# Transposing the rotated q and k by DMA instead of on TensorE, in a gated linear attention with a gated MLP

## Chip, cores, metric

The kernel runs on one core of a Trainium2 chip. The metric is the device time of one execution in microseconds (us), and lower is better. A ratio is the mean time of one kernel's fast runs over the mean time of the fast runs of the kernel before in the same rounds, so it is not quite the ratio of the medians that stand beside it. Profiled executions give "spans", which are about 2 us shorter than the times of the same executions (338.0 against 339.8 us before); shares of a period and the positions of instructions come from them.

## The reference, cut to what matters

The first part is a linear recurrence with complex decay over 768 steps, for 4 batches and 8 heads of width 48. The second part is a gated MLP over the 3072 resulting tokens.

```python
for t in range(S):                                   # S = 768
    S_re, S_im = ar*S_re - ai*S_im + kv, ar*S_im + ai*S_re
    y[:, :, t] = einsum('bhd,bhde->bhe', q[:, :, t], S_re)
x = y as (3072, 384)
out = (sigmoid(x @ w_gate) * (x @ w_val)) @ w_out    # 384 -> 1536 -> 384
```

The kernel works on chunks ("slabs") of 128 tokens of one batch, 24 in all. In a slab the recurrence becomes attention with a triangular mask: q and k are scaled by the accumulated decay and rotated by the accumulated phase, and a score matmul of k by q follows. That matmul contracts over the head's coordinates, so it wants q and k with those coordinates on the partitions, whereas the rotation leaves tokens on the partitions. Hence the transposes.

## The kernel before

Slabs are grouped into ten blocks of 1, 2, 3, 3, 3, 3, 3, 3, 2 and 1. The loads of block i+2, the preparation of block i+1, the attention of block i, the gate matmuls of block i-1 and the output matmuls of block i-2 are interleaved by hand. ACT's order is the program's. A scheduler, which knows only estimated times, decides the order in which the other engines' and the DMA queue's instructions stand. On each engine, and on the SyncE queue that issues the DMAs, instructions then go in that order.

```python
SIZES = [1, 2, 3, 3, 3, 3, 3, 3, 2, 1]

def prep_b(g):                       # rotation: kst and qst of each slab
    ...
        for i, dst in enumerate((ks, qs)):
            nc.vector.tensor_tensor(out=dst..., in0=G.qk[:, 1 - i, s]..., in1=cs..., op=ALU.mult)
        G.qs.append(qs); G.ks.append(ks)

def turn(s, hf):                     # in attn(g): four heads of q and k
    tp = ps_gen.tile([L, 8, L], F16, tag="gen")
    for i in range(4):
        h = hf * 4 + i
        nc.tensor.transpose(tp[:, 4 + i], G.ks[s][:, h], idn_t)
        nc.tensor.transpose(tp[:, i], G.qs[s][:, h], idn_t)
    qkT = patt.tile([L, 8, L], F16, tag="qkT", bufs=5)
    nc.vector.tensor_copy(out=qkT, in_=tp)

def score(s, hf): ...                # reads qkT: sc, then mask
...
for i in range(NG + 2):              # one stage per block
    if i + 2 < NG:
        loads_a(i + 2); loads_q(i + 2)      # 15 DMAs of 192 KB for a block of 3 slabs
    st = [attn(i) first part, outproj(i - 2), prep_a(i + 1)];            merge(*st)
    st = [attn(i) rest, gateval(i - 1), prep_b(i + 1), prep_0(i + 2)];   merge(*st)
```

(Cut and, in the last four lines, shortened.) All loads, and in the changed kernel all DMA transposes, are issued by SyncE. The weights are loaded by GpSimd through another DMA queue.

Of the kernel before, what the change touches and what calls it, by code (L numbers as in the profile page):

```python
# [17 lines left out]
YSC = 2.0**10  # L18
# [4 lines left out]
def kernel(  # L23
# [58 lines left out]

    def cload(shape, dt, src, name):
        t = const.tile(shape, dt, name=name)
        nc.sync.dma_start(t, src.ap())
        return t


    class Grp:
# [22 lines left out]
                    dst.rearrange("t (h d) -> t h d", d=D),  # L112
                    src[b, :, c * L:(c + 1) * L].rearrange("h t d -> t h d"))

    loads_a(0)
    wl_t = cload([L, L], F32, wl_d, "wl_t")
    wt_t = cload([L, L], F32, wt_d, "wt_t")
    on_t = cload([L, L], F32, on_d, "on_t")
    idn_t = cload([L, L], F16, idn_d, "idn_t")
    nid_t = cload([L, L], F16, nid_d, "nid_t")  # L120
    msk_t = cload([L, L], F32, msk_d, "msk_t")
    loads_q(0)
    pio2 = const.tile([L, 1], F32, name="pio2")
    nc.vector.memset(pio2, np.pi / 2)

# [33 lines left out]
    def prep_0(g):  # L159
        G = gs[g]  # L160
        n = len(GROUPS[g])
        G.lm = pa.tile([L, NS, HD], F32, name=f"lm_{g}", tag="lm")
        sq = pa.tile([L, 2, NS, HD], F32, name=f"sq_{g}", tag="sq", bufs=1)
        nc.scalar.activation(out=sq[:, :, :n], in_=G.a2[:, :, :n],  # L164
                             func=FT.Square)
        for s in range(n):
            nc.gpsimd.tensor_tensor(out=G.lm[:, s], in0=sq[:, 0, s],  # L167
                                    in1=sq[:, 1, s], op=ALU.add)
            nc.gpsimd.tensor_scalar(out=G.lm[:, s], in0=G.lm[:, s],
                                    scalar1=CAP, scalar2=-1.0,  # L170
                                    op0=ALU.min, op1=ALU.max)
            yield
        for s in range(n):
            nc.gpsimd.tensor_scalar(out=G.v16[:, s], in0=G.v32[:, s],  # L174
                                    scalar1=YSC, scalar2=1.0,
                                    op0=ALU.mult, op1=ALU.mult)
        yield

    def prep_a(g):
        G = gs[g]  # L180
        n = len(GROUPS[g])
        ar, ai = G.a2[:, 0, :n], G.a2[:, 1, :n]
        lm = G.lm[:, :n]
        nc.scalar.preload_act_table_set("natural_log_exp_and_others")  # L184
        nc.scalar.activation(out=ar, in_=ar, func=FT.Ln)
        nc.scalar.activation(out=lm, in_=lm, func=FT.Ln)
        nc.scalar.activation(out=ar, in_=ar, func=FT.Exp, scale=-1.0)  # L187
        for s in range(n):
            G.last_pool = nc.gpsimd.tensor_tensor(  # L189
                out=G.a2[:, 1, s], in0=G.a2[:, 1, s], in1=G.a2[:, 0, s],  # L190
                op=ALU.mult)
        yield
        for s, (b, c) in enumerate(GROUPS[g]):
            ee = pe_.tile([L, 2, HD], F32, name=f"ee_{g}_{s}", tag="ee")
            cl = ps_gen.tile([L, HD], F32, name=f"cl_{g}_{s}", tag="gen")
            nc.tensor.matmul(cl, wl_t, G.lm[:, s], start=True, stop=True)  # L196
            nc.scalar.activation(out=ee[:, 0], in_=cl, func=FT.Exp,
                                 scale=0.5)
            nc.scalar.activation(out=ee[:, 1], in_=cl, func=FT.Exp,  # L199
                                 scale=-0.5)  # L200
            nc.sync.dma_start(scr[b][c:c + 1], ee[L - 1:L, 0])
            with nc.allow_non_contiguous_dma(reason="column of decays"):
                for p0 in (0, 64):
                    nc.sync.dma_start(
                        rbe[b][p0:p0 + D, c],
                        scr[b][c].rearrange("(h d) -> d h", d=D))
            if c > 0:
                nc.vector.tensor_tensor(
                    out=arr[b][:, c - 1], in0=rbe[b][:, c - 1],
                    in1=rbe[b][:, c], op=ALU.mult)  # L210
            nc.gpsimd.tensor_tensor(out=G.qk[:, :, s], in0=G.qk[:, :, s],  # L211
                                    in1=ee, op=ALU.mult)
            yield

    def prep_b(g):
        G = gs[g]
        n = len(GROUPS[g])
        th = G.a2[:, 1]
        nc.scalar.preload_act_table_set("sigmoid_and_others")
        nc.scalar.activation(out=th[:, :n], in_=th[:, :n], func=FT.Arctan)  # L220
        nc.scalar.preload_act_table_set("silu_and_others")
        G.qs, G.ks = [], []
        yield
        for s, (b, c) in enumerate(GROUPS[g]):
            ct = ps_gen.tile([L, HD], F32, name=f"ct_{g}_{s}", tag="gen")
            nc.tensor.matmul(ct, wt_t, th[:, s], start=True, stop=False,  # L226
                             skip_group_check=True)
            if c > 0:
                nc.tensor.matmul(ct, on_t, run[b], start=False, stop=False,  # L229
                                 skip_group_check=True)  # L230
            if c < NCH - 1:
                nr = psm.tile([L, HD], F32, name=f"run_{g}_{s}", tag="run")
                if c == 0:
                    nc.gpsimd.tensor_copy(out=nr, in_=th[:, s])
                else:
                    nc.gpsimd.tensor_tensor(out=nr, in0=run[b], in1=th[:, s],
                                            op=ALU.add)
                run[b] = nr
            r16 = psm.tile([L, HD], F16, name=f"r16_{g}_{s}", tag="r16")
            nc.vector.tensor_scalar(out=r16, in0=ct, scalar1=RCONST,  # L240
                                    scalar2=-RCONST, op0=ALU.add, op1=ALU.add)
            nc.tensor.matmul(ct, nid_t, r16, start=False, stop=True,
                             skip_group_check=True)
            yield
            cs = pcs.tile([L, 2, HD], F32, name=f"cs_{g}_{s}", tag="cs")
            nc.scalar.activation(out=cs[:, 0], in_=ct, func=FT.Abs)
            nc.scalar.activation(out=cs[:, 1], in_=ct, func=FT.Sin,
                                 scale=TWO_PI)
            nc.scalar.activation(out=cs[:, 0], in_=cs[:, 0], func=FT.Sin,  # L249
                                 scale=-TWO_PI, bias=pio2)  # L250
            qs, ks = slots[(FIRST[g] + s) % NSLOT]
            for i, dst in enumerate((ks, qs)):
                nc.vector.tensor_tensor(  # L253
                    out=dst.rearrange("p h (r x) -> p h r x", r=2)[:, :, :, 0:D],
                    in0=G.qk[:, 1 - i, s].rearrange("p (h d) -> p h d", d=D)
                    .unsqueeze(2).broadcast_to([L, H, 2, D]),
                    in1=cs.rearrange("p r (h d) -> p h r d", d=D),
                    op=ALU.mult)
            G.qs.append(qs)
            G.ks.append(ks)  # L260
            yield
# [4 lines left out]
    def attn(g):  # L266
# [28 lines left out]
                    nc.vector.tensor_copy(out=pn, in_=kv)  # L295
                P[b] = pn

        def turn(s, hf):
            tp = ps_gen.tile([L, 8, L], F16, name=f"tp_{g}_{s}_{hf}",
                             tag="gen")  # L300
            for i in range(4):
                h = hf * 4 + i
                nc.tensor.transpose(tp[:, 4 + i], G.ks[s][:, h], idn_t)  # L303
                nc.tensor.transpose(tp[:, i], G.qs[s][:, h], idn_t)  # L304
            qkT = patt.tile([L, 8, L], F16, name=f"qkT_{g}_{s}_{hf}",
                            tag="qkT", bufs=5)
            nc.vector.tensor_copy(out=qkT, in_=tp)  # L307
            Q[s].append(qkT)

        def score(s, hf):  # L310
            qkT = Q[s][hf]
            sc = ps_gen.tile([L, 4, L], F32, name=f"sc_{g}_{s}_{hf}",
                             tag="gen")
            for i in range(4):
                nc.tensor.matmul(sc[:, i], qkT[:, 4 + i], qkT[:, i],  # L315
                                 start=True, stop=True)
            mst = patt.tile([L, 4, L], F16, name=f"mst_{g}_{s}_{hf}",
                            tag="mst", bufs=5)
# [6 lines left out]
        def yout(s):  # L325
            b, c = GROUPS[g][s]
            y = ps_gen.tile([L, H, D], F32, name=f"y_{g}_{s}", tag="gen")
            for h in range(H):
                if c > 0:
                    nc.tensor.matmul(y[:, h], Q[s][h // 4][:, h % 4],  # L330
                                     X[s][:, h], start=True, stop=False)
                nc.tensor.matmul(y[:, h], M[s][h // 4][:, h % 4], V[s][:, h],  # L332
                                 start=(c == 0), stop=True)
# [11 lines left out]

        for s in range(n + 1):
            if s < n:
                turn(s, 0)
                yield
                turn(s, 1)  # L350
                yield
                state(s)
                yield
# [68 lines left out]
        return len(GROUPS[g])  # L422

    with tc.manual_schedule(engines={ACT}):
        run_all(prep_0(0))
        run_all(prep_a(0))
        loads_a(1)
        loads_q(1)
        with tc.issue_after(gs[0].last_pool.ins):
            load_weights()  # L430
        run_all(prep_b(0))
        run_all(prep_0(1))
        for i in range(NG + 2):
            st = []
            if i + 2 < NG:
# [1 line left out]
                loads_q(i + 2)  # L437
            if i < NG:
                at = attn(i)
                na = 7 * sz(i)  # L440
                n1 = na * 2 // 5
                st.append((take(at, n1), n1))
            if 0 <= i - 2:
# [9 lines left out]
            if i + 1 < NG:  # L453
                st.append((prep_b(i + 1), 1 + 2 * sz(i + 1)))
            if i + 2 < NG:
                st.append((prep_0(i + 2), 1 + sz(i + 2)))
            merge(*st)
# [1 line left out]
_INS = ['q', 'k', 'v', 'a_re', 'a_im', 'moe_w_gate', 'moe_w_val', 'moe_w_out']  # L459
# [26 lines left out]
```

## Time and profile before

339.7 us (median; 339.17 to 340.0).

| | before |
|---|---|
| span | 338.0 us |
| TensorE busy | 268.2 us |
| VectorE / ACT / GpSimd busy | 211.5 / 221.9 / 161.6 us |
| busy time of the DMA queue of SyncE, over 16 engines | 51.7% of the span |

The page's busy line, and two rows of its 40 slices of 8.45 us (tenths of busy time):

```profile
PE 268.2 (79%) x2328; PEld 175.5 (52%) x2328; DVE 211.5 (63%) x385; ACT 221.9 (66%) x377; POOL 161.6 (48%) x177
...
PE   0414073549778997989899989998999999999995
...
DMA  6999999991894199539813960383023100100110
```

The start is bound by loads: DMA at 9 tenths and TensorE mostly idle for about seven slices. From slice 11 or so on TensorE is nearly full. The table of windows says the same in numbers; its columns are the stretch, its length, then each engine's busy time with the number of instructions (PE, weight loads, VectorE, ACT, GpSimd), TensorE's granted clock, the DMA share and GB/s:

```profile
0.00:57.00 57.00, 17.64 (x90) 9.60 (x90) 14.02 (x30) 28.02 (x36) 31.33 (x42) 0.85 1.17 175
...
121.00:154.00 33.00, 29.77 (x257) 18.62 (x256) 25.53 (x45) 25.77 (x43) 20.71 (x23) 1.00 0.76 125
...
187.00:221.00 34.00, 31.66 (x276) 20.07 (x275) 24.86 (x46) 25.73 (x43) 18.84 (x19) 1.00 0.59 101
```

(The DMA share adds up the packets' times, so it can exceed 1.) In the steady stage a period handles one block of three slabs: TensorE is busy 29.8 of 33 us, ACT 25.8. What the transposes cost is less plain. The view of the tile tp, into which the transposes write (in PSUM, the memory for TensorE's results), lists its instructions (duration of one in ns, minimum/median/maximum, first and last start in us, then the forms):

```profile
L303 PE MATMUL tp<-idn_t,kst x192: 216/219/314, 19.0 to 314.7; 128*128 128x128 f16 x192
L304 PE MATMUL tp<-idn_t,qst x192: 217/219/314, 19.9 to 314.7; 128*128 128x128 f16 x192
L307 DVE COPY qkT<-tp x48: 675/688/692, 20.8 to 315.0; 128x1024 f16<-128x1024 f16 x48
```

384 records of 219 ns would be 84 us, but the records overlap. The windows, asked for the tile tp alone, give the time in which at least one of them ran: 33.14 us.

```profile
0.00:338.00 338.00, 33.14 (x384) 32.38 (x48) 0.94 0.59 97
```

ACT's order is fixed by the program, and each block's decay preparation begins there with a table load. These loads are the "marks", and a "stage" runs from one mark to the next; stage i holds the attention of block i. Three marks of the kernel before, from its timeline (start us, us, engine, line):

```profile
52.86 1.28 ACT L184 ACT_TABLE_LOAD   x1
...
90.06 1.28 ACT L184 ACT_TABLE_LOAD   x1
...
256.35 1.28 ACT L184 ACT_TABLE_LOAD   x1
```

They open stages 1, 2 and 7.

### The profile page before, as it was taken

What the parts mean: (1) busy time and instruction counts of PE and PEld (TensorE: products, weight loads), DVE (VectorE), ACT (ScalarE), POOL (GpSimd) and SP (SyncE); (2) the same over time, 40 slices, a digit from 0 to 9 for tenths busy, and PEclk for the clock granted to TensorE, in tenths of its full rate; (3) what the DMA queues carried; (4) which work ended last, traced back from release to release, by engine and by line L of the source; (5) the groups of instructions that cost most, each with busy time, mean ns of one, the idle gap of its engine ahead of it and who ended that gap; (6) DMA issues with size and microseconds to landing.
All of it is one profiled execution on the core that took longest, in us unless ns stands there. A gap on an engine that the chain in (4) does not pass through costs nothing.

```text
span 338.0 us, 6365 instructions
## 1 busy us (share of the span) xinstructions
PE 268.2 (79%) x2328; PEld 175.5 (52%) x2328; DVE 211.5 (63%) x385; ACT 221.9 (66%) x377; POOL 161.6 (48%) x177
## 2 busy tenths in 40 slices
PE   0414073549778997989899989998999999999995
PEld 0102042236556664656566656565666666666874
DVE  2021027528883985797679647966797798476633
ACT  4664067566689489749785977597757865774443
POOL 2880197957189519924873487247602630300000
PEclk9999559759796999999999999999999999999999
DMA  6999999991894199539813960383023100100110
GB/s 141 150 191 186 197 186 131 181 148 26 117 174 63 25 172 186 88 64 186 150 28 64 185 134 19 66 163 57 2 47 95 26 0 20 54 2 23 48 44 28
DMA packets 152382, 32.70 MB, mean 97 GB/s; under 512 B 144904, under 2 KB 152352, under 8 KB 152352
## 3 DMA queue, kind: packets, MB, share of 16 engines
q1 hardware_dynamic: 148368, 28.76, 51.7%
q0 software_dynamic: 3984, 3.54, 6.5%
q8 instruction: 18, 0.29, 0.4%
q14 instruction: 12, 0.10, 0.1%
HBM read 31.07 MB, written 4.76 MB: 106 GB/s over the span
## 4 chain that ended last, share of the span: by engine, by line
PE 48%; ACT 19%; DMA 10%; DVE 7%; POOL 6%; issue 5%; SPq 3%; DVEq 0%; ACTq 0%; POOLq 0%
PE pg L373 10%; PE pv L378 9%; PE po L392 9%; DMA v<-in_v_dram 5%; PE cl L196 4%; PE ct L226 4%; DMA a<-in_a_im_dram 3%; POOL qk L211 3%; PE ct L229 3%; ACT sq L164 2%; ACT g L381 2%; PE tp L304 2%; PE tp L303 2%; DVE qst L253 2%; ACT L184 2%
## 5 line engine op out<-in xcount | busy, mean ns | idle before, releaser
L373 PE MATMUL pg<-xt,wg 128*128 128x384 f16 (+2 forms) x360 | 68.0, 296 | 7.9 <-ACT g L381 5.7
L378 PE MATMUL pv<-xt,wv 128*128 128x384 f16 (+2 forms) x360 | 68.9, 297 | 3.6 <-DVE p L382 2.8
L381 ACT ACTIVATE g<-pg 128x384 f16<-128x384 f32 (+2 forms) x120 | 49.5, 429 | 33.6 <-PE pg L373 29.8
L382 DVE SCALAR_TENSOR_TENSOR p<-g,pv 128x384 f16<-128x384 f16 (+2 forms) x120 | 54.4, 467 | 20.8 <-ACT g L381 17.0
L392 PE MATMUL po<-wo,p 128*128 128x384 f16 x288 | 55.2, 326 | 0.0
L307 DVE COPY qkT<-tp 128x1024 f16<-128x1024 f16 x48 | 32.4, 687 | 33.6 <-PE tp L304 33.3
L373 PEld LDWEIGHTS <-wg 128*128 128x128 f16 x360 | 31.9, 98 | 25.3 <-issue 14.8
L211 POOL TENSOR_TENSOR qk<-qk,ee 128x768 f32<-128x768 f32 x24 | 43.6, 1837 | 2.8 <-ACT ee L199 2.6
L226 PE MATMUL ct<-a,wt_t 128*128 128x384 f32 x48 | 24.6, 599 | 24.0 <-ACT a L220 23.9
L240 DVE TENSOR_SCALAR r<-ct 128x384 f16<-128x384 f32 x24 | 13.2, 551 | 48.3 <-PE ct L229 29.0
L378 PEld LDWEIGHTS <-wv 128*128 128x128 f16 x360 | 32.4, 98 | 19.1 <-issue 7.1
L196 PE MATMUL cl<-lm,wl_t 128*128 128x384 f32 x48 | 24.1, 593 | 19.0 <-DMA qk<-in_k_dram 9.3
L319 DVE TENSOR_TENSOR mst<-sc,msk_t 128x512 f16<-128x512 f32 x48 | 32.4, 684 | 8.3 <-PE sc L315 8.1
L189 POOL TENSOR_TENSOR a<-a 128x384 f32<-128x384 f32 x24 | 23.8, 1015 | 28.7 <-ACT a L187 28.6
L174 POOL TENSOR_SCALAR v<-v 128x384 f16<-128x384 f32 x24 | 15.5, 644 | 43.2 <-PE y L332 25.8
L167 POOL TENSOR_TENSOR lm<-sq 128x384 f32<-128x384 f32 x24 | 25.9, 1095 | 17.6 <-ACT sq L164 17.0
L392 PEld LDWEIGHTS <-p 128*128 128x128 f16 x288 | 26.2, 98 | 13.8 <-issue 0.7
L303 PE MATMUL tp<-idn_t,kst 128*128 128x128 f16 x192 | 29.8, 230 | 2.9 <-DVE kst L253 2.9
L304 PE MATMUL tp<-idn_t,qst 128*128 128x128 f16 x192 | 29.2, 229 | 1.8 <-DVE qst L253 1.8
L285 POOL CAST x<-u 128x384 f16<-128x384 f32 x20 | 11.3, 569 | 33.9 <-DVE u L279 21.4
L253 DVE TENSOR_TENSOR kst<-qk,cs 128x768 f16<-128x768 f32 x24 | 23.7, 988 | 5.4 <-ACT cs L249 4.9
L253 DVE TENSOR_TENSOR qst<-qk,cs 128x768 f16<-128x768 f32 x24 | 26.8, 1119 | 0.0
(54 smaller groups left out, 490.3 us busy)
## 6 DMA issues: line engine op xcount, KB each, us to landing
a<-in_a_re_dram SPq DMA_DIRECT2D x24, 192.0 KB
a<-in_a_im_dram SPq DMA_DIRECT2D x24, 192.0 KB
qk<-in_q_dram SPq DMA_DIRECT2D x24, 192.0 KB
qk<-in_k_dram SPq DMA_DIRECT2D x24, 192.0 KB
v<-in_v_dram SPq DMA_DIRECT2D x24, 192.0 KB
out_dram<-ot SPq DMA_DIRECT2D x24, 192.0 KB
wg<-in_moe_w_gate_dram POOLq DMA_DIRECT2D x3, 384.0 KB, 7.1
wv<-in_moe_w_val_dram POOLq DMA_DIRECT2D x3, 384.0 KB, 8.6
```

Source lines behind the costliest of these rows:

```text
L196: nc.tensor.matmul(cl, wl_t, G.lm[:, s], start=True, stop=True)
L211: nc.gpsimd.tensor_tensor(out=G.qk[:, :, s], in0=G.qk[:, :, s], in1=ee, op=ALU.mult)
L226: nc.tensor.matmul(ct, wt_t, th[:, s], start=True, stop=False, skip_group_check=True)
L253: nc.vector.tensor_tensor(out=dst.rearrange("p h (r x) -> p h r x", r=2)[:, :, :, 0:D], in0=G.qk[:, 1 - i, s].rearrange("p (h d) -> p h d" ...
L303: nc.tensor.transpose(tp[:, 4 + i], G.ks[s][:, h], idn_t)
L304: nc.tensor.transpose(tp[:, i], G.qs[s][:, h], idn_t)
L307: nc.vector.tensor_copy(out=qkT, in_=tp)
L373: nc.tensor.matmul(pg, wg16[:, j, fc], G.xt[:, j, :nt], start=(j == 0), stop=(j == 2))
L378: nc.tensor.matmul(pv, wv16[:, j, fc], G.xt[:, j, :nt], start=(j == 0), stop=(j == 2))
L381: nc.scalar.activation(out=g16, in_=pg, func=FT.Tanh, scale=0.5)
L382: nc.vector.scalar_tensor_tensor(out=G.p[:, fb, :nt], in0=g16, scalar=1.0, op0=ALU.add, in1=pv, op1=ALU.mult)
L392: nc.tensor.matmul(po, G.p[:, fb, s * L:(s + 1) * L], wo16[:, fb], start=(fb == 0), stop=(fb == NFB - 1))
```

## The change

The intent: take 384 matmuls from the engine that binds, and 48 copies of 0.69 us from VectorE, and give the work to the DMA engines, which are idle for long stretches in the later part. In addition, the loads of block 1 go ahead of the weights, and the cast of v moves by a stage.

```diff
-        def turn(s, hf):
-            tp = ps_gen.tile([L, 8, L], F16, ...)
-            for i in range(4):
-                h = hf * 4 + i
-                nc.tensor.transpose(tp[:, 4 + i], G.ks[s][:, h], idn_t)
-                nc.tensor.transpose(tp[:, i], G.qs[s][:, h], idn_t)
-            qkT = patt.tile([L, 8, L], F16, ..., bufs=5)
-            nc.vector.tensor_copy(out=qkT, in_=tp)
+        def turn(s):
+            for x, src in ((1, G.ks[s]), (0, G.qs[s])):
+                t = patt.tile([L, H, L], F16, ..., tag=f"qkT{x}", bufs=3)
+                nc.sync.dma_start_transpose(
+                    out=t, in_=src.rearrange("p h x -> p (h x)"))
+                Q[s].insert(0, t)
...
     with tc.manual_schedule(engines={ACT}):
+        nc.scalar.preload_act_table_set("natural_log_exp_and_others")
+        loads_a(0)
+        consts()
+        loads_q(0)
+        loads_a(1)
+        loads_q(1)
         run_all(prep_0(0))
         run_all(prep_a(0))
-        loads_a(1)
-        loads_q(1)
-        with tc.issue_after(gs[0].last_pool.ins):
-            load_weights()
         run_all(prep_b(0))
         run_all(prep_0(1))
+        with tc.issue_after(gs[1].last_pool.ins):
+            load_weights()
```

(Cut: the cast of v from `prep_0` to `prep_b`, score and yout reading the new tiles, step counts; `consts()`, which now issues the loads of the constants; and `last_pool`, which now marks the last GpSimd instruction on a block's squares instead of its decay products.)

More of the change, by code (lines that the diff above doesn't have):

```diff
@@ L84, in cload, with consts @@
         t = const.tile(shape, dt, name=name)
-        nc.sync.dma_start(t, src.ap())
+        CONSTS.append((t, src))
         return t
+    CONSTS = []
+    def consts():
+        for t, src in CONSTS:
+            nc.sync.dma_start(t, src.ap())
     class Grp:
@@ L113, in loads_q @@
                     src[b, :, c * L:(c + 1) * L].rearrange("h t d -> t h d"))
-    loads_a(0)
     wl_t = cload([L, L], F32, wl_d, "wl_t")
@@ L121 @@
     msk_t = cload([L, L], F32, msk_d, "msk_t")
-    loads_q(0)
     pio2 = const.tile([L, 1], F32, name="pio2")
@@ L168, in prep_0 @@
                                     in1=sq[:, 1, s], op=ALU.add)
-            nc.gpsimd.tensor_scalar(out=G.lm[:, s], in0=G.lm[:, s],
+            G.last_pool = nc.gpsimd.tensor_scalar(
+                                    out=G.lm[:, s], in0=G.lm[:, s],
                                     scalar1=CAP, scalar2=-1.0,
@@ L172, in prep_0 @@
             yield
-        for s in range(n):
-            nc.gpsimd.tensor_scalar(out=G.v16[:, s], in0=G.v32[:, s],
-                                    scalar1=YSC, scalar2=1.0,
-                                    op0=ALU.mult, op1=ALU.mult)
-        yield
     def prep_a(g):
@@ L188, in prep_a @@
         for s in range(n):
-            G.last_pool = nc.gpsimd.tensor_tensor(
+            nc.gpsimd.tensor_tensor(
                 out=G.a2[:, 1, s], in0=G.a2[:, 1, s], in1=G.a2[:, 0, s],
@@ L222, in prep_b @@
         G.qs, G.ks = [], []
+        for s in range(n):
+            nc.gpsimd.tensor_scalar(out=G.v16[:, s], in0=G.v32[:, s],
+                                    scalar1=YSC, scalar2=1.0,
+                                    op0=ALU.mult, op1=ALU.mult)
         yield
@@ L296, in state @@
                 P[b] = pn
-        def turn(s, hf):
-            tp = ps_gen.tile([L, 8, L], F16, name=f"tp_{g}_{s}_{hf}",
-                             tag="gen")
-            for i in range(4):
-                h = hf * 4 + i
-                nc.tensor.transpose(tp[:, 4 + i], G.ks[s][:, h], idn_t)
-                nc.tensor.transpose(tp[:, i], G.qs[s][:, h], idn_t)
-            qkT = patt.tile([L, 8, L], F16, name=f"qkT_{g}_{s}_{hf}",
-                            tag="qkT", bufs=5)
-            nc.vector.tensor_copy(out=qkT, in_=tp)
-            Q[s].append(qkT)
+        def turn(s):
+            for x, src in ((1, G.ks[s]), (0, G.qs[s])):
+                t = patt.tile([L, H, L], F16, name=f"qkT_{g}_{s}_{x}",
+                              tag=f"qkT{x}", bufs=3)
+                nc.sync.dma_start_transpose(
+                    out=t, in_=src.rearrange("p h x -> p (h x)"))
+                Q[s].insert(0, t)
         def score(s, hf):
-            qkT = Q[s][hf]
             sc = ps_gen.tile([L, 4, L], F32, name=f"sc_{g}_{s}_{hf}",
@@ L314, in score @@
             for i in range(4):
-                nc.tensor.matmul(sc[:, i], qkT[:, 4 + i], qkT[:, i],
+                h = 4 * hf + i
+                nc.tensor.matmul(sc[:, i], Q[s][1][:, h], Q[s][0][:, h],
                                  start=True, stop=True)
@@ L329, in yout @@
                 if c > 0:
-                    nc.tensor.matmul(y[:, h], Q[s][h // 4][:, h % 4],
+                    nc.tensor.matmul(y[:, h], Q[s][0][:, h],
                                      X[s][:, h], start=True, stop=False)
@@ L347, in attn @@
             if s < n:
-                turn(s, 0)
-                yield
-                turn(s, 1)
+                turn(s)
                 yield
@@ L439 @@
                 at = attn(i)
-                na = 7 * sz(i)
+                na = 6 * sz(i)
                 n1 = na * 2 // 5
@@ L455 @@
             if i + 2 < NG:
-                st.append((prep_0(i + 2), 1 + sz(i + 2)))
+                st.append((prep_0(i + 2), sz(i + 2)))
             merge(*st)
```

## The prediction

> **What bounds it now.** The table of windows shows two stages. From 0 to 57 us the DMA engines are saturated (about 175 GB/s) and TensorE is busy only 17.6 us; the chain of waits runs there through loads: the v load of block 1, stretched by the weight loads to 18.4 us (19.4 to 37.8), then VectorE/GpSimd preparation, then a_im of block 2 (42.7 to 47.3). From about 90 us TensorE binds: busy 29.8, 31.1, 31.7 and 33.0 us in periods of 33, 33, 34 and 35 us (121 to 256), against ACT 25 to 26, DVE 25 to 27, GpSimd 16 to 21. (A period is three slabs.)
>
> **Removed.** 384 TensorE transposes and 48 VectorE copies of 687 ns. The groups credit the transposes with 59 us, but their two lines overlap: the windows of that tile alone sum to 33.1 us. So about 4.1 us of TensorE and 4.1 us of VectorE per period go.
>
> **Added.** 48 SBUF-to-SBUF transposes of 256 KB (128x1024, 2 bytes) on the SyncE queue. No trace here has one. The Trainium skill, "DMA: Bandwidth & Descriptors", Latency and other measured facts, gives 261 GB/s for a DMA transpose: estimate 1.0 us each, like the 1.0 us that a 192 KB load occupies here. "VectorE: DVE Perf Modes", The three transpose paths, gives 1309 ns for one 128x128 block, so eight blocks may well take more; my own middle estimate is 1.5 to 3 us of queue time each. Per period that is 9 to 18 us beside a DMA share of 0.6 to 0.76 (20 to 25 us of 33). The queue issues in order, and the built program puts twelve loads between the first and later transposes of a block, so scores of slabs 1 and 2 can wait. DMA or its queue will be nearly full until the loads end at about 240 us, and free afterwards.
>
> **Moved.** Weights start after block 1's squares, not after block 0's preparation: block 1 should have v and q by about 18 us rather than 41. Block 2's loads then meet the weights, so its a lands perhaps only 3 to 5 us earlier than 47. The v cast moves one stage later (about neutral).
>
> **On the critical path.** Start: 5 to 9 us. Steady stage: six full periods and the smaller ones could give 25 to 30 us if TensorE stayed the bound; I expect half or less, because DMA, its in-order queue or ACT (26 us busy plus handovers) takes over: periods of 30 to 32 us while loads run, 29 to 30 after. The last block exposes one transpose latency.
>
> Sum: 340 − 7 − 12 + 3 = about 324 us. Range 300 to 352. Faster by over 2%: 0.60; within: 0.21; slower: 0.19.
>
> **What would show each step.** TensorE busy falls by 30 to 36 us; DVE by 32. The page's DMA share in the middle slices rises to 8 or 9 tenths until about slice 28. Waits: the score matmuls' weight loads wait for a DMA (none now), some microseconds each. The first ct of block 1 starts near 20 us, not 44.
>
> **What would make it wrong.** If a transpose takes 1 us or less with its issue, TensorE keeps its bound and the time is near 305. If it takes over 4 us, or the SyncE queue spends that long issuing it, six per period plus 27 other transfers exceed 33 us, loads come late, and the kernel is slower, past 350. If the scheduler's order makes TensorE wait behind late scores (in-order engine), the saved 4 us come back as waits.

## The result, and the profile after

349.18 us (median; 348.97 to 349.9) against 339.7 us: ratio 1.0284, 95% interval 1.0264 to 1.0305. The result is correct, and the kernel is slower by 2.8%. The granted TensorE clock is not the cause: it was 0.902 in the profiled run of the change and 0.939 before, but the change's three other runs had 0.949 to 0.951 and still took 348.97 to 349.34 us.

The page after, the same three lines:

```profile
PE 247.8 (71%) x1944; PEld 155.2 (45%) x1944; DVE 179.1 (51%) x337; ACT 220.3 (63%) x377; POOL 159.8 (46%) x177
...
PE   0330002534686598869996998699989999999996
...
DMA  6999999998239989987997599839937923500500
```

TensorE lost 268.2 - 247.8 = 20.4 us of work and VectorE 32.4 us, so the intent was met. But TensorE now has a hole in slices 4 to 6, and the stages show when time was lost. The same marks, after:

```profile
66.94 1.28 ACT L184 ACT_TABLE_LOAD   x1
...
108.23 1.28 ACT L184 ACT_TABLE_LOAD   x1
...
271.58 1.28 ACT L184 ACT_TABLE_LOAD   x1
```

By the mark at the head of stage 2 the change is 108.23 - 90.06 = 18.2 us behind. From there to the head of stage 7 it takes 163.4 us where the kernel before took 166.3, so it wins back 2.9. From there to the end it takes 76.5 in place of 81.7 and wins 5.1 more. The three add up to the difference of the spans, 10.1 us.

So the steady stage is not the place. The list of TensorE's waits (waiter, what ended the wait, us in total, times, longest) names the new one; no score matmul waited for a DMA before:

```profile
PE sc L315 <- DMA qkT<-qst: 45.6, 6, 33.0
```

One wait of 33 us. The chain of waits through it, in order of time (start, us, what; SPq is SyncE's queue issuing, L105 and L117 are loads, L306 a transpose):

```profile
24.12 5.53 SPq L105
...
29.75 6.15 SPq L117
...
35.94 5.06 SPq L117
...
41.05 4.25 SPq L117
...
53.35 2.05 SPq L306
...
55.46 3.13 DMA qkT<-qst
...
58.63 0.58 PE sc L315 x4
```

And the rotated k and q of block 0 had been ready since 18.5 us, by the timeline of VectorE (in brackets its wait before, and for what):

```profile
16.68 0.96 DVE L257 TENSOR_TENSOR kst<-qk,cs 128x768 f16<-128x768 f32 x1 [2.04 <-ACT cs L253]
17.55 0.95 DVE L257 TENSOR_TENSOR qst<-qk,cs 128x768 f16<-128x768 f32 x1
```

They waited 35 us to be transposed, because the queue had the fifteen loads of block 2 to issue first. Four of these took 4 to 6 us each, while the weights were being loaded (their packets move from 23.7 to 47.9 us in the trace); the last five before the transposes took about 1 us each. The second transpose itself, once issued at 55.46, was there 3.1 us later. Meanwhile TensorE stood before the scores of block 0 and did not do the phase matmuls of block 1 that stand behind them: ACT had finished their input at 31.5 us, and they ran at 59.0, right after the first scores. This trace shows TensorE taking its matmuls in order.

The Trainium skill, "DMA: Bandwidth & Descriptors", Anatomy of one DMA, says where such a wait sits: the DMA engines do not wait on semaphores, and any wait happens on the issuing sequencer before it hands the DMA over. (The section describes DMAs that GpSimd issues; these are SyncE's.) This trace agrees: SyncE's own list of waits has 51.4 us of transposes waiting for the rotation of k, and everything behind them on the queue waits along. In the order of one queue a load can hold up a transpose, and a transpose can hold up a load.

### The profile page after: what moved, and what is told of

The parts are those of the page before. It is cut to its first block, busy times and chain, and to the rows that moved or that the text cites. A ratio compares the mean times of both kernels' runs of the same rounds, so it can differ in the third digit from the quotient of the medians.

```text
span 348.1 us, 5629 instructions
## 1 busy us (share of the span) xinstructions
PE 247.8 (71%) x1944; PEld 155.2 (45%) x1944; DVE 179.1 (51%) x337; ACT 220.3 (63%) x377; POOL 159.8 (46%) x177
## 2 busy tenths in 40 slices
DMA packets 203068, 45.24 MB, mean 130 GB/s; under 512 B 195592, under 2 KB 203040, under 8 KB 203040
## 3 DMA queue, kind: packets, MB, share of 16 engines
q1 hardware_dynamic: 199056, 41.35, 72.5%
## 4 chain that ended last, share of the span: by engine, by line
PE 41%; ACT 22%; SPq 14%; DVE 8%; issue 7%; DMA 7%; DVEq 0%; ACTq 0%
PE pv L376 8%; SPq L117 8%; PE pg L371 8%; PE po L390 7%; PE ct L230 5%; PE cl L196 4%; DMA qkT<-qst 3%; PE ct L233 3%; SPq L306 2%; ACT L219 2%; SPq L105 2%; ACT L184 2%; ACT g L379 2%; ACT L379 2%; DVE qst L257 2%
## 5 line engine op out<-in xcount | busy, mean ns | idle before, releaser
L371 PE MATMUL pg<-xt,wg 128*128 128x384 f16 (+2 forms) x360 | 70.3, 303 | 16.5 <-ACT g L379 11.0
L376 PE MATMUL pv<-xt,wv 128*128 128x384 f16 (+2 forms) x360 | 70.1, 302 | 2.4 <-ACT ot L396 1.4
L379 ACT ACTIVATE g<-pg 128x384 f16<-128x384 f32 (+2 forms) x120 | 48.4, 428 | 24.4 <-PE pg L371 21.6
L319 DVE TENSOR_TENSOR mst<-sc,msk_t 128x512 f16<-128x512 f32 x48 | 32.7, 684 | 52.3 <-PE sc L315 52.2
L315 PE MATMUL sc<-qkT,qkT 128*128 128x128 f16 x192 | 19.3, 229 | 45.6 <-DMA qkT<-qst 45.6
L390 PE MATMUL po<-wo,p 128*128 128x384 f16 x288 | 51.3, 326 | 0.0
L371 PEld LDWEIGHTS <-wg 128*128 128x128 f16 x360 | 33.5, 100 | 35.8 <-issue 22.7
L315 PEld LDWEIGHTS <-qkT 128*128 128x128 f16 x192 | 15.0, 103 | 58.6 <-DMA qkT<-kst 41.0
L196 PE MATMUL cl<-lm,wl_t 128*128 128x384 f32 x48 | 25.1, 620 | 17.2 <-ACT lm L186 17.2
L189 POOL TENSOR_TENSOR a<-a 128x384 f32<-128x384 f32 x24 | 23.7, 1012 | 11.7 <-ACT a L187 11.1
L335 ACT ACTIVATE y<-y 128x384 f16<-128x384 f32 x24 | 11.8, 492 | 26.9 <-PE y L332 26.7
L224 POOL TENSOR_SCALAR v<-v 128x384 f16<-128x384 f32 x24 | 13.0, 542 | 30.7 <-PE y L332 25.4
L168 ACT ACTIVATE sq<-a 128x2304 f32<-128x2304 f32 (+2 forms) x10 | 17.4, 1738 | 15.3 <-DMA a<-in_a_im_dram 15.3
L250 ACT ACTIVATE cs<-ct 128x384 f32<-128x384 f32 x24 | 11.9, 495 | 23.9 <-PE ct L246 23.9
```

Of the source, the lines that this page charges most:

```text
L196: nc.tensor.matmul(cl, wl_t, G.lm[:, s], start=True, stop=True)
L315: nc.tensor.matmul(sc[:, i], Q[s][1][:, h], Q[s][0][:, h], start=True, stop=True)
L319: nc.vector.tensor_tensor(out=mst, in0=sc, in1=msk_t.unsqueeze(1).broadcast_to([L, 4, L]), op=ALU.mult)
L371: nc.tensor.matmul(pg, wg16[:, j, fc], G.xt[:, j, :nt], start=(j == 0), stop=(j == 2))
L376: nc.tensor.matmul(pv, wv16[:, j, fc], G.xt[:, j, :nt], start=(j == 0), stop=(j == 2))
L379: nc.scalar.activation(out=g16, in_=pg, func=FT.Tanh, scale=0.5)
```

## The experiments

Three theories were told apart. Q: the loss is queue order, since transposes stand behind loads. C: the loss is the DMA work itself, 12.5 MB more through the DMA engines. L: the loss comes from the new order of loads and weights.

### The two halves of the change

Load order alone: `turn`, its two steps and the step count of the kernel before, everything else as in the change.

> The new load order, the later weights and the moved v cast alone; transposes stay on TensorE. Theory Q (queue order: the loss of the change is block 0's transposes standing behind block 2's loads on the SyncE queue): 328 to 338 us, with no wait over 5 us of the score matmuls. Theory L (the later weights cost the time by themselves): 345 us or more. Theory C (DMA work of the transposes): says nothing against 328 to 338.

Measured: 338.7 us, ratio 0.998 (0.9956 to 1.0003), no difference. L falls. The load order also brings almost nothing: the mark of stage 1 comes 6.4 us earlier (46.5 against 52.9), that of stage 2 only 2.3 us (87.8 against 90.1), and the span is 1.0 us shorter.

Transposes alone: the kernel before with the new `turn`.

> The DMA transposes alone, loads and weights in the old order. Theory Q: block 0's transposes still stand behind block 2's loads, which end at about 53 us in both orders, so TensorE still waits near 20 us or more for the first scores: 343 to 355 us. Theory L: about 333 to 338 us, since the order is the old one. Theory C: 345 to 355 us, with the loss spread over all periods rather than before 108 us.

Measured: 346.58 us, ratio 1.0213 (1.0172 to 1.0255). Its mark of stage 2 is at 106.7 us, and one score wait of 29.5 us stands in its list. So it is the transposes, and the time goes in the first stages, as Q says and C does not.

### What was to be had at most

```diff
-            for x, src in ((1, G.ks[s]), (0, G.qs[s])):
-                ...
+            Q[s][:] = [G.qs[s], G.ks[s]]     # no transposes, wrong result
```

> Wrong result on purpose: the changed kernel with no transposes at all, scores read the rotated q and k as they lie. The most that removing them could give. Theory Q: 305 to 325 us. If it is 335 us or more, the TensorE transposes were hidden behind other work in the kernel before and there was nothing to gain.

Measured: 322.93 us, ratio 0.9517 (0.9479 to 0.9556), result wrong. Against the load order alone this is 338.7 - 322.9 = 15.8 us. That is the whole value of the transposes on TensorE and their copies. In the five stages from 2 to 6 it is 9.2 us (167.6 against 158.4), 1.8 us per stage. TensorE sheds 23.4 us of busy time in the whole run (271.3 against 247.9), and two thirds of it reach the clock.

### Same bytes, other place in the queue

```diff
 def prep_b(g):
     ...
             G.ks.append(ks)
+            pair = []
+            for x, src in ((1, ks), (0, qs)):
+                t = patt.tile([L, H, L], F16, ..., tag=f"qkT{x}", bufs=4)
+                nc.sync.dma_start_transpose(
+                    out=t, in_=src.rearrange("p h x -> p (h x)"))
+                pair.insert(0, t)
+            G.T.append(pair)
 def turn(s):
-    ...
+    Q[s][:] = G.T[s]
```

(Cut: five buffers of rotated q instead of six, to make room.)

> The changed kernel with each slab's transposes issued at once after its rotation (a stage earlier), ahead of the loads of the block after next; qkT has 4 buffers, the q slots are 5 of 6 to make room. Same bytes, same load order. Theory Q: the 33 us wait of the first scores is gone, 318 to 332 us. Theory C: the same DMA work must be done, so 342 to 352 us. Theory L: 345 us or more.

Measured: correct, 326.31 us, ratio 0.9614 (0.959 to 0.9638). It beats both kernels. The built program now has every transpose of block i ahead of all loads of block i+2, apart from a few lines at the end. Its first two transposes go out as soon as the data is rotated (queue's timeline):

```profile
18.32 1.45 SPq L270 DMA_TRANSPOSE qkT<-kst  x1
19.88 1.25 SPq L270 DMA_TRANSPOSE qkT<-qst  x1
```

C falls. The DMA engines carry the same 45.24 MB in the same 203068 packets as in the change. They are even fuller, because the run is shorter. The windows from 120 to 150 us, first of this kernel and then of the one with no transposes:

```profile
120.00:150.00 30.00, 26.14 (x211) 15.87 (x208) 20.55 (x37) 24.79 (x41) 18.66 (x19) 1.00 0.99 155
```

```profile
120.00:150.00 30.00, 26.35 (x208) 15.73 (x207) 20.77 (x38) 23.95 (x41) 20.79 (x23) 1.00 0.64 108
```

The DMA share goes from 0.64 to 0.99 (over all of stages 2 to 6 from 0.60 to 1.01), and the engines do the same work in the same time. The marks of stages 2 and 7, first of the early kernel and then of the one with no transposes:

```profile
90.22 1.28 ACT L185 ACT_TABLE_LOAD   x1
...
248.52 1.28 ACT L185 ACT_TABLE_LOAD   x1
```

```profile
86.90 1.28 ACT L184 ACT_TABLE_LOAD   x1
...
245.30 1.28 ACT L184 ACT_TABLE_LOAD   x1
```

From the mark of stage 2 to that of stage 7 the early kernel takes 158.3 us and the one without transposes 158.4. In the steady stage the DMA transposes, placed well, cost nothing that shows. The 3.2 us between the two spans lie before stage 2 (90.2 against 86.9).

Against the change the early kernel saves 348.1 - 324.7 = 23.4 us of span: 18.0 before stage 2, 5.1 in stages 2 to 6, 0.3 after. It also has four buffers of each transposed tile where the change has three. That is not what gains the 18.0: a kernel further down with three buffers and blocks 0 to 4 early keeps pace with it as far as the head of stage 5 (184.5 against 184.7 us).

### Is it block 0? A theory that fell

The 33 us wait was that of block 0, so I relieved only that one: its two transposes early, all others as in the change.

> The changed kernel with only block 0's two transposes issued early (behind block 1's loads, ahead of block 2's); all others stay where the change has them. Theory Q: the start is repaired and the steady stage is not, so 328 to 334 us, the 33 us wait gone. Theory C (the DMA work of the transposes is what costs): two transposes of 48 cannot matter, 345 us or more.

Measured: 348.99 us, ratio 1.0285 (1.0243 to 1.0326). No gain, although the wait of 33 us is gone. Q in this form falls, and C had forecast the number, but the early kernel had already spoken against C. The trace says where the loss went. The list of waits up to 125 us, then the queue:

```profile
PE sc L329 <- DMA qkT<-qst: 16.9, 1, 16.9
```

```profile
73.50 1.20 SPq L117 DMA_DIRECT2D v<-in_v_dram  x1
75.15 1.67 SPq L320 DMA_TRANSPOSE qkT<-kst  x1
```

Now block 1's transposes stand behind the loads of block 3, and its stage takes 52.3 us in place of the early kernel's 35.2.

Starting the weights later, so that block 2's loads should run at full speed, was meant as a test of the other half of the wait, the slow loads ahead:

> The changed kernel with the weight loads started later (gate and value weights after block 1's decay products, output weights after block 2's). Block 0's transposes still stand behind block 2's loads, but those no longer share the DMA engines with the weights. Theory Q with the slow loads as its second half: block 2's loads end near 33 us, the first scores wait about 15 us instead of 33, total 332 to 342 us. If the length of the loads ahead does not matter: 347 to 352 us.

Measured: 348.43 us, ratio 1.0246 (1.0214 to 1.0278): a miss. The first score wait fell to 25.1 us and the mark of stage 1 came at 59.4 instead of 66.9 us, but stage 1 then took 48.6 us instead of 41.3, and by stage 2 nothing was left of the gain (107.96 against 108.23). The edit reached its aim only in part. The weights' packets began at 27.8 us in place of 23.7, still among block 2's loads. A v load of block 2 waited 7.5 us for the cast of block 1's v, which stood behind the weights' issues on GpSimd, and a later load took 4.3 us beside the weights. So what the slow loads cost by themselves stays open.

### The loss moves

Two candidates were left: R, the delay hurts only in the first blocks, where TensorE has little else to do; and S, it moves on to the next block that is not relieved.

> The run with block 0 alone early was no faster than the change, because block 1's transposes (issued at 75 us behind block 3's nine loads) then held TensorE 17 us. So theory Q is restated as R: every block's transposes stand behind the loads of the block after next, and the delay is paid in the first blocks, where TensorE has little other work (no gate matmuls yet for block 0, 128 and 256 tokens for blocks 1 and 2), and mostly hidden afterwards. Here blocks 0 and 1 (3 of 24 slabs) are early. R: 329 to 338 us. Rival S (the loss moves on whole to the next block, whichever is not relieved): 345 us or more.

Measured: 344.62 us, ratio 1.0144 (1.0114 to 1.0174), well above R and 0.4 us short of S. Blocks 0 and 1 are as fast as in the early kernel (mark of stage 2 at 89.9), then stage 2 takes 45.8 us where the early kernel takes 32.4. The queue's last load of block 4 and first transpose of block 2, and TensorE's score that waits for it:

```profile
98.55 1.15 SPq L117 DMA_DIRECT2D v<-in_v_dram  x1
99.75 2.08 SPq L320 DMA_TRANSPOSE qkT<-kst  x1
```

```profile
105.34 0.59 PE L329 MATMUL sc<-qkT,qkT 128*128 128x128 f16 x4 [14.58 <-DMA qkT<-qst]
```

The same with blocks 0 and 1 transposed on TensorE. A first try was not built, for want of on-chip memory (SBUF). Its expectation:

> The changed kernel with the slabs of the first two blocks (3 of 24) transposed on TensorE as before, the rest by DMA. Theory Q: 326 to 334 us, as no early score waits for the queue. Theory C: 343 us or more, since 21 of 24 slabs still go through the DMA engines.

And that of the one that ran:

> Blocks 0 and 1 (3 of 24 slabs) transposed on TensorE, the rest by DMA in the place of the change (a second label: under the first an older file was refused by the build). R: within 3 us of the run with blocks 0 and 1 early, 328 to 338 us, since what matters is that no early score stands in the queue, not which unit transposes. Theory C (DMA work of the transposes) or S: 343 us or more.

Measured: 340.42 us, ratio 1.0037 (1.0016 to 1.0057), above R's 338 and below S's 343, so a miss for both. Stage 2 takes 45.7 us, just as with the early transposes, although the first three slabs do not use the DMA at all.

Only block 1 early:

> Only block 1's transposes early, block 0's behind block 2's loads as in the change. R: block 0's scores still wait until about 58 us, which delays block 1's rotation to about 67 us, but its transposes then go at once instead of at 75 to 81: 336 to 345 us. If block 1's place alone decides: 329 to 334 us. S: 345 us or more.

Measured: 350.14 us, ratio 1.0321 (1.029 to 1.0352), as S had it. It pays twice: stage 0 takes 48.4 us (36.8 in the early kernel), because block 0 is held up, and stage 2 takes 44.5, because block 2 is.

Blocks 2 to 9 early, 0 and 1 as in the change:

> The opposite of the first: blocks 2 to 9 early, blocks 0 and 1 as in the change. The markers of the full early run give 18 us lost before the third full block and 5 us after it. R: only the 5 us come back, 341 to 346 us. If the later blocks carry the loss: 326 to 334 us.

Measured: 345.56 us, ratio 1.0181 (1.0161 to 1.0201), inside R's range. The start's loss stays (mark of stage 2 at 107.5), and of the steady loss 3.2 us come back: stages 2 to 6 take 160.2 us, between the change's 163.4 and the early kernel's 158.3. (This kernel has three buffers of the transposed tiles, the early one four; whether that makes the last 1.9 us was not tried.)

The decisive one moves the loss to a place where TensorE has full work:

> Blocks 0 to 4 early, block 5 the first whose transposes stand behind the loads (nine of block 7) in the built order. With blocks 0 and 1 early the stage of block 2 took 45.8 us instead of 32.4 and later stages were normal again. S (a one-time shift: the first block whose transposes stand behind the loads of the block after next waits for them once, and from then on the loads run ahead by that much): the stages up to block 4 as in the full early run, one stage of 40 to 47 us at block 5, total 334 to 343 us. R (once TensorE has gate matmuls of full blocks to do, the delay hides): no stage over 36 us, 326 to 331 us.

Measured: 339.01 us, ratio 0.9998 (0.9948 to 1.0047). The span is 337.2 - 324.7 = 12.5 us longer than the early kernel's, and a single stage holds it. Its two marks in the timeline, and the wait between them:

```profile
184.53 1.28 ACT L184 ACT_TABLE_LOAD   x1
...
229.33 1.28 ACT L184 ACT_TABLE_LOAD   x1
```

```profile
PE sc L329 <- DMA qkT<-qst: 9.6, 1, 9.6
```

Stage 5 takes 44.8 us against 31.8. R, which allowed no stage over 36 us, falls, and S holds in the form that it had here. Block 5's first k and q were rotated at about the same time in both kernels (the q from 175.2 us here, from 175.4 in the early kernel), and then the first transpose of block 5 was issued, here and in the early kernel:

```profile
194.35 2.04 SPq L320 DMA_TRANSPOSE qkT<-kst  x1
```

```profile
177.69 1.25 SPq L270 DMA_TRANSPOSE qkT<-kst  x1
```

Of the 13.0 us that stage 5 takes longer, 9.6 are the wait shown; the rest was not traced.

The stages side by side, in us (from the marks; "rest" is from the mark of stage 8 to the end; the longest excess over the early kernel in bold):

| kernel | 0 | 1 | 2 | 3 | 4 | 5 | 6 | 7 | rest |
|---|---|---|---|---|---|---|---|---|---|
| early, all blocks | 36.8 | 35.2 | 32.4 | 30.9 | 31.2 | 31.8 | 32.0 | 26.9 | 49.3 |
| the change | **49.0** | 41.3 | 30.2 | 32.2 | 34.4 | 35.0 | 31.5 | 26.9 | 49.6 |
| block 0 early | 37.0 | **52.3** | 30.2 | 32.1 | 33.9 | 35.0 | 31.6 | 26.9 | 49.7 |
| blocks 0, 1 early | 36.9 | 35.1 | **45.8** | 31.1 | 32.2 | 34.9 | 31.5 | 27.8 | 49.5 |
| blocks 0 to 4 early | 37.0 | 35.8 | 30.3 | 32.2 | 31.2 | **44.8** | 31.6 | 26.9 | 49.4 |

The bold stages of the partly relieved kernels exceed the early kernel's by 17.1, 13.4 and 13.0 us, so the loss does not move on whole, as S first had it: it gets smaller, but it does not go.

The order in which the built programs put the queue's instructions explains the one bold stage per row. Here is the queue around it, told in my own short form (L3 is all loads of block 3, T1 the transposes of block 1, T2.0 those of its first slab and T2.1k that of k alone in its second; a, v and q are the loads of one array, q standing for q and k):

```
the change:        ... L2 | T0 | v3 a3 q3 | T1 | v4 a4 | T2.0 T2.1k | q4 | ... | v5 | T3.0 | a5 | ...
block 0 early:     ... T0 | L2 L3 | T1 | v4 a4 | T2.0 T2.1k | q4 | ...
blocks 0, 1 early: ... T1 | L3 L4 | T2 | v5 a5 | T3.0 T3.1 | q5 | ...
blocks 0-4 early:  ... T4 | L6 L7 | T5 | v8 | T6.0 | a8 | ...
all early:         ... T0 | L2 | T1 | L3 | T2 | L4 | T3 | L5 | ...
```

In each kernel the first blocks whose transposes are not early stand behind all the loads of the block after next, and they wait for these: once in the partly relieved kernels, in blocks 0 and 1 in the change. After that the order opens: transposes of a first slab go ahead of part of the next loads. So it is a delay that is paid once, where the order changes from one pattern to the other, and not a price per transpose. The smaller loss of the change in its steady stage (5.1 us) fits the pattern that follows, in which some of a block's transposes stand behind the six q and k loads of the block after next. That the run with blocks 2 to 9 early won back 3.2 of it agrees; it was not tried apart.

### A try at more

The early transposes with the weights started later (gate and value weights after block 1's decay products, output weights a block later).

> The early transposes together with the later weights; a try at a better kernel. In the run with early transposes block 2's a arrives at 53.6 us and ACT stalls for it. With the weights behind it, it should arrive near 32 us: 316 to 324 us. If the weights then come too late for the first gate matmuls, 326 us or more.

Measured: correct, 324.37 us, ratio 0.9553 (0.9513 to 0.9592), 0.4 us past the slow end of what was expected of it. Block 2's data does come earlier (mark of stage 1 at 39.6 instead of 55.0 us), but stage 1 is then 47.6 us long, and 3.0 us are left at stage 2. It is the fastest correct kernel. It and the early kernel were timed in different rounds and their intervals touch, so that it is the faster of the two is likely and not settled.

## Why the prediction was wrong, point by point

The sum was "340 − 7 − 12 + 3 = about 324 us", with a range of 300 to 352 and 0.60 for faster. The measured 349.18 us lies inside the range, but the sign was wrong. In spans: 338.0 + 18.2 (start) - 2.9 (stages 2 to 6) - 5.1 (after) gives the 348.1 of the change up to rounding. Everything after the start came to -8.0 where the sum had -12 + 3, so nearly the whole error lies in one term, the start: -7 was forecast, +18.2 came.

- **The step that failed: "Start: 5 to 9 us" of gain.** It was a loss of 18.2 us. The prediction said of the queue that "the built program puts twelve loads between the first and later transposes of a block, so scores of slabs 1 and 2 can wait". That is the order in the middle blocks, and the sum gave it no cost at the start. In blocks 0 and 1 all transposes stand behind the loads of the block after next, so that TensorE waited 33.0 us for those of block 0, and the built order, which was at hand, showed it. "The first ct of block 1 starts near 20 us" failed with it: it ran at 59.0 us in the change, since the waiting score stood before it on TensorE. In the early kernel it ran at 31.7, as soon as ACT had its input, so about 12 us of this miss have nothing to do with the place of the transposes.
- **The gain of the load order**, −7 by itself, was mis-sized too: measured alone, 1.0 us.
- **"about 4.1 us of TensorE ... per period go"** was mis-sized. TensorE's busy time fell by 20.4 us in the change, not by the 33.1 of the windows, because records of other matmuls run beside the transposes' records, and that time stays when the transposes go: counted from the records of the trace before, a transpose ran with no other matmul beside it in 17.2 of the 33.1 us. The Trainium skill, "Perfetto Trace Analysis", Identifying the Most-Contended Engine, says that matmul busy time does not tell well how close TensorE is to its limit, since pipelined instructions look smaller in the trace. A neighbouring trap: the busy time of one group, 33.1 us, is not what its removal saves, 20.4. VectorE's 32 us was right: 32.4.
- **The critical share** ("25 to 30 us if TensorE stayed the bound; I expect half or less") was about right in size: with no transposes at all the gain was 15.8 us, and the early kernel got 339.2 - 326.3 = 12.9 us of medians from the two parts together. The reason given was right only in part. Periods of 30 to 32 us came (30.9 to 32.4 in the early kernel), but the DMA engines and their queue do not set them, since they are as long with no transposes at all. Whether ACT does was not tried.
- **The cost of a transpose**, "1.5 to 3 us of queue time each", was right at its low end for DMA time, and its consequence was wrong. SyncE's queue is busy 72.5% of 348.1 us against 51.7% of 338.0, so (252.4 - 174.7) / 48 = 1.6 us of all 16 engines each, and the issue takes 1.24 to 1.28 us (median). But the "DMA ... nearly full" that it foresaw did not lengthen the stages: at a share of 1.01 stages 2 to 6 were as long as at 0.60.
- **The failure clause** "If the scheduler's order makes TensorE wait behind late scores" is what happened. It was listed, and it was given too little weight: the longest such wait was 33 us, not the 4 us per period that it spoke of.

## What to carry to other kernels

When work moves from a compute engine to a DMA queue that also issues prefetches, find in the built order what stands ahead of the new transfers in each of the first blocks as well as in a middle one; a transfer whose data is ready behind a block of prefetches waits for all of them, and in-order engines wait with it. Issue the transfer where its data is produced, ahead of the next prefetches: the same bytes then went from +2.8% to -3.9%. When relieving one instance of such a delay brings nothing, see whether the delay has moved to the next instance before dropping the theory.

## What the Trainium skill lacked or had wrong

- "DMA: Bandwidth & Descriptors", Latency and other measured facts, gives 261 GB/s for a DMA transpose with a non-contiguous middle dimension, and 350 to 400 for a contiguous one. Here a 256 KB SBUF-to-SBUF transpose took 1.6 us of the 16 engines' time, which is 262144 B / 1.62 us = 162 GB/s, counted while loads shared the engines. The last one of the early kernel, after the loads had ended, took 1.4 us from its first packet to its last, about 185 GB/s.
- "VectorE: DVE Perf Modes", The three transpose paths, gives 1309 ns for one 128x128 block by DMA and nothing for many blocks in one instruction. Here eight blocks in one instruction were issued in 1.24 to 1.28 us (median), and one of them was there 3.1 us after its issue began.
- No page gives the issue time on SyncE of such a transpose on this chip; "DMA: Bandwidth & Descriptors" has only counts of sequencer cycles for "previous generations" in a comparison with a later chip. The 1.24 to 1.28 us measured here are three times the 0.43 us of a plain load issued with nothing in its way.
- "DMA: Bandwidth & Descriptors", Rules for kernel authors, advises to issue a DMA early and wait late, and does not say that early loads on a queue hold up a later transfer on which the next result depends. Here that cost 18 us at the start.
